# Loading V to every fourth partition, and ordering the score rows to match, in an attention kernel

## Chip, cores and metric

One core of a Trainium2 chip. The metric is device time in microseconds (us) of the whole kernel. Ratios compare runs of the same rounds on the same chip.

## The reference

Plain softmax attention over B x H = 512 heads, with 192 queries, 1024 keys and head dimension 128, all in bfloat16:

```python
B, H, Sq, Sk, D = 16, 32, 192, 1024, 128
def reference(q, k, v):
    scale = q.shape[-1] ** -0.5
    scores = jnp.einsum("bhqd,bhkd->bhqk", q, k) * scale
    p = jax.nn.softmax(scores, axis=-1)
    return jnp.einsum("bhqk,bhkd->bhqd", p, v)
```

q, k and v are normal numbers times 0.05, so the scores are tiny and each softmax row is nearly flat.

## The kernel before

The kernel works on pairs of heads; there are 256 pairs. Inputs come from HBM (the chip's main memory) into tiles in SBUF (on-chip memory of 128 partitions); the tensor engine writes its results to PSUM (a second on-chip memory). The scores are computed transposed, keys on the partitions, so the exponentials can serve directly as stationary operands of the second matmul. For that, the keys on the partitions of the scores and the rows of V on the partitions of V must be in the same order. One queue (SP) issues all transfers in a fixed order. K, q and the reordered V have four slots each (R = 4), V as loaded has ten (NVS = 10).

```python
    def load_k(p):
        if p >= R:
            e.wait_ge(s_tr, 2 * (p - R) + 2)
        e.dma_start(
            kn[:, p % R, :],
            kf[2 * p:2 * p + 2].rearrange("x (m s) d -> (x m) (s d)", s=2 * T),
        ).then_inc(s_kn[p % R], 16)
    def load_v(p):
        if p >= NVS:
            e.wait_ge(s_pv, p - NVS + 1)
        for w in range(2):
            e.dma_start(
                vs[64 * w: 64 * w + 64, p % NVS, :, :],
                vf[2 * p:2 * p + 2].rearrange("x (m w t) d -> w m x (t d)", w=2, t=T)[w],
            ).then_inc(s_v[p % NVS], 16)
# ... the loop that issues transfers, after a head that loads K and q of 4 pairs and V of 10
    for n in range(NPR + 2):
        if n + R < NPR:
            load_k(n + R)
            load_q(n + R)
        if n >= 2 and n - 2 + NVS < NPR:
            load_v(n - 2 + NVS)
        if n >= 3 and (n - 2) % GP == 0:
            store((n - 2) // GP - 1)
```

A partition of `kn` holds 16 rows of K, 4 KB. A partition of `vs` holds 8 rows of V, 2 KB for each head: transfer w = 0 of a pair fills partitions 0 to 63, w = 1 fills 64 to 127. POOL (GpSimd) copies V to a padded tile, with a column of ones for the row sums. The tensor engine transposes K in half steps (y = 0, 1), DVE (VectorE) copies each half out of PSUM, and one step of the tensor engine is two half steps of scores, transposes and the second matmul:

```python
    for p in range(NPR):
        gp.wait_ge(s_v[p % NVS], 32 * (p // NVS + 1))
        if p >= R:
            gp.wait_ge(s_pv, p - R + 1)
        gp.tensor_copy(
            vp[:, p % R, :, 0:D].bitcast(U32),
            vs[:, p % NVS, :, :].rearrange("p x (t d) -> p (x t) d", d=D).bitcast(U32),
        ).then_inc(s_vp, 1)
# ... tensor engine; `take` waits for a semaphore and counts it back
    def tr(p, y):
        if y == 0:
            take(s_kn[p % R], 16)
        if (p, y) != (0, 0):
            take(s_ev, 1)
        ins = None
        for t in range(T):
            for z in range(2):
                c0 = (8 * y + t) * D + 64 * z
                ins = pe.transpose(
                    k_ps[64 * z: 64 * z + 64, t * 128: t * 128 + 128],
                    kn[:, p % R, c0: c0 + 64], ident[:], tile_position=(0, 64 * z))
        ins.then_inc(s_tr, 1)
# ... inside qk(h), scores of one head
        for t in range(T):
            cut = {2: (0, 2, 3), 5: (0, 1, 3)}.get(t, (0, 3))
            for j0, j1 in zip(cut[:-1], cut[1:]):
                mv = qt[:, p % R, j0:j1, 64 * x: 64 * x + 64]
                c0 = t * SQ + j0 * 64
                for w in range(2):
                    ins = pe.matmul(
                        S[64 * w: 64 * w + 64, c0: c0 + (j1 - j0) * 64],
                        kt[:, p % R, 8 * w + t, 64 * x: 64 * x + 64], mv,
                        start=True, stop=True, tile_position=(0, 64 * w))
    def step(n):
        for x in range(2):
            if n < NPR:
                qk(2 * n + x)
            if n + 1 + x < NPR:
                tr(n + 1 + x, 1 - x)
            if n >= 2:
                pv(n - 2, 12 * x, 12 * x + 12)
```

## Time and profile before

| | before |
|---|---|
| time, median of the first 3 runs | 1199.38 us (1196.12 to 1203.05) |
| span of the profiled run, mean granted clock (share of TensorE's full clock) | 1197.7 us, 0.988 |
| PE (TensorE) busy | 995.0 us, 83% |
| ACT (ScalarE), DVE, POOL busy | 744, 546, 268 us |
| PE waiting ahead of the transposes of K | 186.0 us |

From the profile's page of the kernel before: busy time of each engine, then busy tenths in 40 equal slices of the span (DMA is the mean of the 16 DMA engines), then two groups of instructions (busy time and mean length of one, then idle time before them and what ended it), then the transfers (number, size, median us from issue to landing).

```profile
...
PE 995.0 (83%) x30722; PEld 947.9 (79%) x30722; DVE 546.4 (46%) x1031; ACT 744.1 (62%) x513; POOL 268.1 (22%) x263
...
PE   4598888888888888888888888888888888888885
...
DMA  9999999999999999999999999999999999999991
GB/s 211 230 257 264 284 264 279 277 273 277 282 278 268 277 271 279 275 278 272 280 278 274 277 279 266 281 279 267 285 277 269 284 272 274 275 271 277 274 294 40
...
L656 DVE COPY f_kt<-f_k 128x1024 bf16<-128x1024 bf16 x512 | 354.2, 692 | 623.6 <-PE f_k L569 623.5
L569 PE MATMUL f_k<-f_ident,f_kn 128*64 128x128 bf16 x8192 | 331.2, 221 | 186.2 <-PEq L558 186.0
...
f_kn<-in_k_dram SPq DMA_DIRECT2D x256, 512.0 KB, 9.9
f_vs<-in_v_dram SPq DMA_DIRECT2D x512, 256.0 KB, 9.2
...
```

PE has 17% of the span idle, and nearly all of it stands ahead of line 569, the transposes of K. PE's sequencer is named as the releaser, since a separate `take` on it waits for the K load. The DMA slices read 9 tenths throughout.

The view of waits says the same in totals (engine and line, what it waited for: us in total, times, longest):

```profile
...
PE f_k L569 <- PEq L558: 186.0, 245, 17.6
POOL f_vp L549 <- DMA f_vs<-in_v_dram: 18.6, 4, 9.3
...
```

In the timeline of PE (start, length, instructions; in brackets the idle time before), a half step is scores, transposes, second matmul:

```profile
...
602.54 0.86 PE L590 MATMUL f_s<-f_qt,f_kt 128*64 128x192 bf16 x20
603.21 0.64 PE L569 MATMUL f_k<-f_ident,f_kn 128*64 128x128 bf16 x16
603.65 0.90 PE L608 MATMUL f_o<-f_vp,f_pt 128*64 128x129 bf16 x24
604.36 0.86 PE L590 MATMUL f_s<-f_qt,f_kt 128*64 128x192 bf16 x20
605.55 0.64 PE L569 MATMUL f_k<-f_ident,f_kn 128*64 128x128 bf16 x16 [0.33 <-PEq L558]
605.99 0.90 PE L608 MATMUL f_o<-f_vp,f_pt 128*64 128x129 bf16 x24
606.69 0.86 PE L590 MATMUL f_s<-f_qt,f_kt 128*64 128x192 bf16 x20
...
```

The half step that starts at 602.54 runs without a wait and ends at 604.36: 1.82 us, so about 3.65 us for an undisturbed step of one pair (two half steps). In the next, the transposes start 0.5 us late. Over the span a pair takes 1197.7 / 256 = 4.68 us.

In a steady stretch, as a table by stretch (us of the stretch; busy us and instructions of PE, its weight loads, DVE, ACT, POOL; granted clock; DMA share; GB/s):

```profile
...
60.00:360.00 300.00, 259.35 (x8100) 247.77 (x8094) 142.84 (x269) 195.95 (x136) 69.94 (x67) 1.00 1.07 274
...
```

The trace also records every DMA packet with its size and duration, and sizes tell the streams apart: q 256 B, output 768 B, V 2 KB, K 4 KB. Sums are divided by 16 engines.

| stream | packets | MB | sum / 16, us | median ns |
|---|---|---|---|---|
| V | 65,536 | 134.2 | 628.5 | 159 |
| K | 32,768 | 134.2 | 407.4 | 164 |
| q | 98,304 | 25.2 | 110.9 | 18 |
| output | 32,768 | 25.2 | 88.9 | 36 |

V costs 1.54 times what K costs for the same bytes, at 134.2 MB / 628.5 us = 214 GB/s.

### The profile page before, as it was taken

The page shows a single profiled execution, that of the slowest core. Times are in us where ns is not written, and L with a number is a line of the kernel's source. Part 1 is how long each engine was busy: PE and PEld are TensorE (multiplying, and loading weights), DVE is VectorE, ACT ScalarE, POOL GpSimd, SP SyncE. Part 2 cuts the span into 40 slices and gives each one's busy share as a digit, 9 for nine tenths or more (in the row PEclk, how much of TensorE's full clock was granted, in tenths as well). Part 3 has the DMA queues.
Part 4 walks back from the last instruction along what each step waited for, and adds up shares of the span by engine and source line. Part 5 has one row for each costly group of instructions (what it writes and reads, how often), then busy time and mean ns, then how long its engine had stood idle before and what let it go on. Part 6 is the DMA issues. An engine that isn't in the chain of part 4 may idle for free. (4 is left out here: it accounts for less than half of the span.)

```text
span 1197.7 us, 67883 instructions
## 1 busy us (share of the span) xinstructions
PE 995.0 (83%) x30722; PEld 947.9 (79%) x30722; DVE 546.4 (46%) x1031; ACT 744.1 (62%) x513; POOL 268.1 (22%) x263
## 2 busy tenths in 40 slices
PE   4598888888888888888888888888888888888885
PEld 3598888887888887887887887787887887878885
DVE  1254444444444444444444444444444444444443
ACT  3276666666666666666666665666666666666663
POOL 1122222222222222222222222222222222222220
PEclk9799999999999999999999999999999999999999
DMA  9999999999999999999999999999999999999991
GB/s 211 230 257 264 284 264 279 277 273 277 282 278 268 277 271 279 275 278 272 280 278 274 277 279 266 281 279 267 285 277 269 284 272 274 275 271 277 274 294 40
DMA packets 250932, 319.39 MB, mean 267 GB/s; under 512 B 119808, under 2 KB 152576, under 8 KB 250880
## 3 DMA queue, kind: packets, MB, share of 16 engines
q1 hardware_dynamic: 250880, 318.85, 104.6%
q8 instruction: 13, 0.21, 0.1%
q14 instruction: 39, 0.32, 0.1%
HBM read 268.44 MB, written 25.17 MB: 245 GB/s over the span
## 5 line engine op out<-in xcount | busy, mean ns | idle before, releaser
L707 ACT ACTIVATE f_pt<-f_s 128x1536 bf16<-128x1536 f32 x512 | 742.8, 1451 | 439.2 <-PE f_s L590 439.2
L656 DVE COPY f_kt<-f_k 128x1024 bf16<-128x1024 bf16 x512 | 354.2, 692 | 623.6 <-PE f_k L569 623.5
L569 PE MATMUL f_k<-f_ident,f_kn 128*64 128x128 bf16 x8192 | 331.2, 221 | 186.2 <-PEq L558 186.0
L549 POOL COPY f_vp<-f_vs 128x1024 uint32<-128x1024 uint32 x256 | 267.2, 1044 | 908.9 <-PE f_o L608 890.3
L608 PE MATMUL f_o<-f_vp,f_pt 128*64 128x129 bf16 x12288 | 459.3, 221 | 2.2 <-PEq L558 2.2
L569 PEld LDWEIGHTS f_k<-f_ident,f_kn 128*64 128x64 bf16 x8192 | 276.1, 110 | 232.1 <-issue 232.0
L590 PE MATMUL f_s<-f_qt,f_kt 128*64 128x192 bf16 (+2 forms) x10240 | 444.4, 231 | 5.2 <-issue 5.2
L608 PEld LDWEIGHTS f_o<-f_vp,f_pt 128*64 128x64 bf16 x12288 | 395.8, 110 | 2.7 <-issue 2.7
L590 PEld LDWEIGHTS f_s<-f_qt,f_kt 128*64 128x64 bf16 x10240 | 360.4, 111 | 5.7 <-issue 5.7
L671 DVE TENSOR_TENSOR f_ob<-f_o,f_rinv 128x384 bf16<-128x384 f32 x256 | 142.7, 557 | 8.9
L667 DVE RECIPROCAL f_rinv<-f_o 128x3 f32<-128x3 f32 x256 | 46.3, 181 | 11.0 <-PE f_o L608 8.5
L707 ACT ACT_TABLE_LOAD x1 | 1.3, 1283 | 0.8 <-PEq L733 0.8
L640 PE MATMUL f_o<-f_bad,f_ones 128*1 128x1 bf16 x1 | 0.2, 164 | 1.4 <-DVEq L696 1.4
L640 PEld LDWEIGHTS f_o<-f_bad,f_ones 128*1 128x1 bf16 x1 | 0.1, 79 | 1.6 <-DVEq L696 1.6
L680 DVE TENSOR_TENSOR f_chk<-f_chk,f_rinv 128x750 f32<-128x750 f32 (+1 forms) x2 | 1.1, 558 | 0.1
L681 DVE TENSOR_REDUCE f_bad<-f_chk 128x1 bf16<-128x750 f32 (+1 forms) x2 | 1.1, 555 | 0.1
L679 DVE TENSOR_SCALAR f_chk<-f_rinv 128x750 f32<-128x750 f32 (+1 forms) x2 | 1.0, 509 | 0.0
L541 POOL TENSOR_SCALAR_AFFINE_SELECT f_ident<-f_ones 128x128 bf16<-128x128 bf16 x1 | 0.3, 294 | 0.1
L698 DVE CAST redo<-f_o 1x1 int32<-1x1 f32 x1 | 0.1, 146 | 0.3 <-PE f_o L641 0.3
L539 POOL MEMSET f_ones<- 128x128 bf16 x1 | 0.2, 205 | 0.3 <-POOLq L733 0.3
L544 POOL MEMSET f_vp<- 128x128 bf16 x1 | 0.2, 213 | 0.0
L733 POOL MEMSET const-float32-0.0<- 128x1 f32 x1 | 0.1, 99 | 0.3 <-issue 0.3
(5 smaller groups left out, 0.5 us busy)
## 6 DMA issues: line engine op xcount, KB each, us to landing
f_kn<-in_k_dram SPq DMA_DIRECT2D x256, 512.0 KB, 9.9
f_vs<-in_v_dram SPq DMA_DIRECT2D x512, 256.0 KB, 9.2
out_dram<-f_ob SPq DMA_DIRECT2D x64, 384.0 KB, 9.5
f_qt<-in_q_dram SPq DMA_TRANSPOSE x256, 9.9
```

The lines of the kernel that those rows point to most:

```text
L549: gp.tensor_copy(vp[:, p % R, :, 0:D].bitcast(U32), vs[:, p % NVS, :, :].rearrange("p x (t d) -> p (x t) d", d=D).bitcast(U32),).then_inc( ...
L569: ins = pe.transpose(k_ps[64 * z: 64 * z + 64, t * 128: t * 128 + 128], kn[:, p % R, c0: c0 + 64], ident[:], tile_position=(0, 64 * z))
L590: ins = pe.matmul(S[64 * w: 64 * w + 64, c0: c0 + (j1 - j0) * 64], kt[:, p % R, 8 * w + t, 64 * x: 64 * x + 64], mv, start=True, stop=True ...
L608: ins = pe.matmul(o_ps[64 * x: 64 * x + 64, j * 129: j * 129 + 129], pt[:, (2 * p + x) % NP, t * SQ + j * 64: t * SQ + j * 64 + 64], vp[:, ...
L640: pe.matmul(o_ps[0:1, 0:1], ones[:, 0:1], bad[:, 0:1], start=True, stop=False)
L656: dve.tensor_copy(kt[:, p % R, 8 * y: 8 * y + 8, :], k_ps[:].rearrange("d (t c) -> d t c", c=128),).then_inc(s_ev, 1)
L667: dve.reciprocal(ri, O[:, :, 128]).then_inc(s_rc, 1)
L671: dve.tensor_tensor(ob[:, so, a, :].rearrange("p (j d) -> p j d", j=3), O[:, :, 0:128], ri.unsqueeze(2).to_broadcast([128, 3, D]), ALU.mul ...
L679: done(dve.tensor_scalar(chk[:, lo:hi], rinv[:, lo:hi], 1.0 / RS_HI, 1.0 / RS_LO, ALU.max, ALU.min))
L680: done(dve.tensor_tensor(chk[:, lo:hi], chk[:, lo:hi], rinv[:, lo:hi], ALU.not_equal))
L681: done(dve.tensor_reduce(bad[:, i: i + 1], chk[:, lo:hi], mybir.AxisListType.X, ALU.max))
L707: act.activation(pt[:, h % NP, :], s_ps[h % 2][:], ACT_FN.Exp, scale=scale).then_inc(s_exp, 1)
```

## The change

The intent: each transfer of V should reach partitions all over the SBUF instead of one half of them. V comes in units of two pairs (four heads). Transfer c of four writes partitions c, c+4, ..., c+124, so partition 4m+2a+b holds the 8 rows from 32m+16b+8a. K stays loaded in 4 KB pieces. For its columns to follow this order, a transpose writes its 64 keys of one head as 32 pairs of neighbouring bfloat16 columns, each pair 8 bytes from the next. Number and size of packets, number of transfers, and all instruction counts of PE, DVE, ACT and POOL stay as they are.

```diff
# ... (hunks that only rename constants are left out)
@@ -453,10 +453,10 @@
 
             kn = sb("f_kn", [128, R, 2 * T * D], BF16)
 
-            kt = sb("f_kt", [128, R, 2 * T, 128], BF16)
+            kt = sb("f_kt", [128, R, T, 2, 128], BF16)
             qt = sb("f_qt", [128, R, 3, 128], BF16)
 
-            vs = sb("f_vs", [128, NVS, 2, T * D], BF16)
+            vs = sb("f_vs", [128, NV2, 4, T * D], BF16)
             vp = sb("f_vp", [128, R, 2 * T, VB], BF16)
             pt = sb("f_pt", [128, NP, T * SQ], BF16)
             ob = sb("f_ob", [128, NSO, GP, 3 * D], BF16)
@@ -489,14 +489,15 @@
                         qf[2 * p:2 * p + 2].rearrange("g (p j) d -> (g p) (j d)", j=3),
                     ).then_inc(s_q[p % R], 16)
 
-                def load_v(p):
-                    if p >= NVS:
-                        e.wait_ge(s_pv, p - NVS + 1)
-                    for w in range(2):
+                def load_v(u):
+                    if u >= NV2:
+                        e.wait_ge(s_pv, 2 * (u - NV2) + 2)
+                    for c in range(4):
                         e.dma_start(
-                            vs[64 * w: 64 * w + 64, p % NVS, :, :],
-                            vf[2 * p:2 * p + 2].rearrange("x (m w t) d -> w m x (t d)", w=2, t=T)[w],
-                        ).then_inc(s_v[p % NVS], 16)
+                            vs[c:128:4, u % NV2, :, :],
+                            vf[4 * u:4 * u + 4].rearrange(
+                                "x (m b a t) d -> a b m x (t d)", b=2, a=2, t=T)[c // 2, c % 2],
+                        ).then_inc(s_v[u % NV2], 16)
 
                 def store(g):
                     so = g % NSO
@@ -519,15 +520,15 @@
                 for p in range(2, R):
                     load_k(p)
                     load_q(p)
-                    load_v(p - 1)
-                for p in range(R - 1, min(NVS, NPR)):
-                    load_v(p)
+                for u in range(1, min(NV2, NPR // 2)):
+                    load_v(u)
                 for n in range(NPR + 2):
                     if n + R < NPR:
                         load_k(n + R)
                         load_q(n + R)
-                    if n >= 2 and n - 2 + NVS < NPR:
-                        load_v(n - 2 + NVS)
+                    u = (n - 3) // 2 + NV2
+                    if n >= 3 and n % 2 == 1 and u < NPR // 2:
+                        load_v(u)
                     if n >= 3 and (n - 2) % GP == 0:
                         store((n - 2) // GP - 1)
                 store(NPR // GP - 1)
@@ -543,12 +544,14 @@
                 ).then_inc(s_set, 1)
                 gp.memset(vp[:, :, :, D:VB], 1.0).then_inc(s_set, 1)
                 for p in range(NPR):
-                    gp.wait_ge(s_v[p % NVS], 32 * (p // NVS + 1))
+                    u, x = divmod(p, 2)
+                    if x == 0:
+                        gp.wait_ge(s_v[u % NV2], 64 * (u // NV2 + 1))
                     if p >= R:
                         gp.wait_ge(s_pv, p - R + 1)
                     gp.tensor_copy(
                         vp[:, p % R, :, 0:D].bitcast(U32),
-                        vs[:, p % NVS, :, :].rearrange("p x (t d) -> p (x t) d", d=D).bitcast(U32),
+                        vs[:, u % NV2, 2 * x: 2 * x + 2, :].rearrange("p x (t d) -> p (x t) d", d=D).bitcast(U32),
                     ).then_inc(s_vp, 1)
 
             @block.tensor
@@ -563,11 +566,14 @@
                     if (p, y) != (0, 0):
                         take(s_ev, 1)
                     ins = None
-                    for t in range(T):
+                    for i in range(8):
+
+                        kp = k_ps[:, 256 * (i % 4): 256 * (i % 4) + 256].rearrange(
+                            "d (m a b) -> d m a b", a=2, b=2)
                         for z in range(2):
-                            c0 = (8 * y + t) * D + 64 * z
+                            c0 = (8 * (i // 4) + 4 * y + i % 4) * D + 64 * z
                             ins = pe.transpose(
-                                k_ps[64 * z: 64 * z + 64, t * 128: t * 128 + 128],
+                                kp[64 * z: 64 * z + 64, :, i // 4, :],
                                 kn[:, p % R, c0: c0 + 64], ident[:], tile_position=(0, 64 * z))
                     ins.then_inc(s_tr, 1)
 
@@ -589,7 +595,7 @@
                             for w in range(2):
                                 ins = pe.matmul(
                                     S[64 * w: 64 * w + 64, c0: c0 + (j1 - j0) * 64],
-                                    kt[:, p % R, 8 * w + t, 64 * x: 64 * x + 64], mv,
+                                    kt[:, p % R, t, x, 64 * w: 64 * w + 64], mv,
                                     start=True, stop=True, tile_position=(0, 64 * w))
                     ins.then_inc(s_qk, 1)
 
@@ -654,8 +660,8 @@
                     if p >= R:
                         dve.wait_ge(s_qk, 2 * (p - R) + 2)
                     dve.tensor_copy(
-                        kt[:, p % R, 8 * y: 8 * y + 8, :],
-                        k_ps[:].rearrange("d (t c) -> d t c", c=128),
+                        kt[:, p % R, 4 * y: 4 * y + 4, :, :],
+                        k_ps[:].rearrange("d (t x c) -> d t x c", x=2, c=128),
                     ).then_inc(s_ev, 1)
 
                 def onorm(p):
```

More of the change, by code (lines that the diff above doesn't have):

```diff
@@ L393, in _ @@
                     exp_first(u)
+HINT = False
 RS_LO = 2.0 ** -40
@@ L399, with _attention_kernel @@
 PE_LOOP = 4
-HINT = False
-def _attention_kernel(nc, q, k, v, out, NVS=10):
+def _attention_kernel(nc, q, k, v, out, NV2=5):
     B, H, SQ, D = q.shape
@@ L431, in _attention_kernel @@
         s_q = [sem("f_q%d" % i) for i in range(R)]
-        s_v = [sem("f_v%d" % i) for i in range(NVS)]
+        s_v = [sem("f_v%d" % i) for i in range(NV2)]
         s_st = [sem("f_st%d" % i) for i in range(NSO)]
```

## The prediction

> **What bounds the kernel now: the DMA engines, through K.** In the page's slices DMA is at 9 tenths or more throughout (q1: 104.6% of 16 engines' span), PE busy 83%. In the view of waits PE stands 186 us, nearly all ahead of the transposes of K (line 569), waiting for a K load. In the timeline an unstalled step of one pair takes about 3.65 us; the span over 256 pairs is 4.68. ACT needs 2.9 us per pair (2 x 1.45), DVE 2.1, POOL 1.04: none binds.
>
> **Where the DMA time goes.** The trace's packets, summed over 16 engines: V 628 us (65,536 of 2 KB, median 159 ns), K 407 us (32,768 of 4 KB, median 164), q 111, output 89. The same 134 MB cost V 1.54 times what they cost K. A pair's V load lasts 2.27 us (median; 230 GB/s), its K load 1.71. [...] The K packets after V took 310 to 340 ns [...]; a K load after an output took 159 ns throughout (about 410 GB/s). [...]
>
> **What the change does.** Each V transfer writes 32 partitions, four apart, over the whole 0..127[...]. Bytes, packets and number of transfers stay, as do the counts on PE, DVE, ACT, POOL. V comes as 1 MB per two pairs; buffers hold ten pairs as before. The transposes write pairs of columns 8 bytes apart in PSUM instead of a solid run; unstalled, 16 issue in 0.42 us now. [...]
>
> **Cost.** If V ran like clean K, 80 ns per packet: V 1.3 us and K 1.3 [...], q 0.38, output 0.35: an estimate of 3.3 us of DMA per pair, below PE's 3.65. Then PE bounds: 256 x 3.65 + some 30 us of head and tail + a few stalls: about 975. [...]
>
> **Prediction: 1005 us, 80% range 962 to 1190.** Faster by over 2%: 0.80; within 2%: 0.15; slower: 0.05.
>
> **What would show it.** Right: V packets' median near 80 ns, V under 420 us of 16 engines; K's slow group (300 ns and over) gone; PE's wait ahead of line 569 from 186 us to under 50; DMA slices below 9 tenths; PE over 95% busy. Transposes: 16 still in 0.42 us, DVE copy 692 ns.
>
> **What would make it wrong.** V packets stay near 159 ns ([...] a limit on the HBM side, the source being now 2 KB every 8 KB): no change. Transposes at half speed: +0.84 us per pair on PE, near 1190. A lower granted clock with busier PE (0.988 now). The 1 MB bursts of V holding K back in the one queue.

The sum is V 1.3 + K 1.3 + q 0.38 + output 0.35 = 3.3 us of DMA per pair (80 ns is half of the 159 that a 4 KB packet of K took after an output; a q load lasted 0.37 us in the trace, though q's packets sum to 0.43 per pair), below PE's 3.65; so 256 x 3.65 = 934 us, with head, tail and stalls about 975. Cut after it are two slower cases: half of the gain, with V 1.8 and K 1.45, so 4.0 us per pair and some 1050 us, and no gain, 1195. They lifted the forecast from 975 to 1005 us and the top of its range to 1190. How likely they were, and that the new order of the columns would cost little, were guesses.

## More of the kernel before

The batches of experiments ran on different chips, so figures from the profiles (packets, waits) are also set side by side across chips; the kernel before took 1199.07 to 1199.85 us (medians) on all of them.

In the one V load that I followed, at 600.8 us, the first 64 of its 256 packets took 84 ns each and the rest 118 to 247 (median 166); the first 32 K packets after it took 313 to 358 ns.

## The result

| | before | after |
|---|---|---|
| time, median | 1199.53 us (4 runs) | 988.26 us (986.07 to 993.17, 4 runs) |
| ratio, 95% interval | | 0.8244 [0.8205, 0.8283] |
| span, granted clock | 1197.7 us, 0.988 | 986.6 us, 0.992 |
| PE busy | 995.0 us, 83% | 948.6 us, 96% |
| V packets: sum / 16, median | 628.5 us, 159 ns | 396.7 us, 86 ns |
| K packets: sum / 16, median | 407.4 us, 164 ns | 366.5 us, 160 ns |
| K packets of 300 ns and over | 6,072 | 977 |
| output packets: sum / 16, median | 88.9 us, 36 ns | 125.3 us, 36 ns |

The same lines from the page of the kernel after:

```profile
...
PE 948.6 (96%) x30722; PEld 944.2 (96%) x30722; DVE 546.1 (55%) x1031; ACT 744.2 (75%) x513; POOL 267.9 (27%) x263
...
PE   4699999999999999999999999999999999999995
...
DMA  9899999999999999999999999999999999999981
GB/s 272 240 287 342 356 328 334 336 355 332 343 325 350 332 337 347 338 344 316 335 353 343 328 331 358 335 345 322 342 319 357 319 354 341 334 326 351 342 263 38
...
L662 DVE COPY f_kt<-f_k 128x1024 bf16<-128x1024 bf16 x512 | 354.0, 691 | 412.8 <-PE f_k L575 412.8
...
L575 PE MATMUL f_k<-f_ident,f_kn 128*64 128x128 bf16 x8192 | 330.5, 220 | 22.8 <-PEq L561 22.7
...
f_kn<-in_k_dram SPq DMA_DIRECT2D x256, 512.0 KB, 5.7
f_vs<-in_v_dram SPq DMA_DIRECT2D x512, 256.0 KB, 4.5
...
```

PE reads 9 tenths in nearly every slice, and its idle time ahead of the transposes (now line 575) fell from 186.2 to 22.8 us. One transpose still takes 220 ns, one DVE copy 691 ns. Landing times about halved (K 9.9 to 5.7 us, V 9.2 to 4.5). But the DMA slices still read 9 tenths.

The waits:

```profile
...
PE f_k L575 <- PEq L561: 22.7, 15, 10.3
POOL f_vp L552 <- DMA f_vs<-in_v_dram: 16.3, 2, 10.6
...
```

Of the 22.7 us, 10.3 are one wait in the head, before 31 us, which stays. Between 50 and 950 us the sum is 2.3.

The timeline of PE:

```profile
...
601.88 0.86 PE L596 MATMUL f_s<-f_qt,f_kt 128*64 128x192 bf16 x20
602.55 0.64 PE L575 MATMUL f_k<-f_ident,f_kn 128*64 128x128 bf16 x16
603.02 0.89 PE L614 MATMUL f_o<-f_vp,f_pt 128*64 128x129 bf16 x24
603.73 0.86 PE L596 MATMUL f_s<-f_qt,f_kt 128*64 128x192 bf16 x20
604.39 0.64 PE L575 MATMUL f_k<-f_ident,f_kn 128*64 128x128 bf16 x16
604.84 0.90 PE L614 MATMUL f_o<-f_vp,f_pt 128*64 128x129 bf16 x24
605.54 0.86 PE L596 MATMUL f_s<-f_qt,f_kt 128*64 128x192 bf16 x20
...
```

No bracket is left. From 601.88 to 605.54 a whole step takes 3.66 us, the length of an undisturbed step of before. The steady stretch:

```profile
...
60.00:360.00 300.00, 299.50 (x9783) 298.94 (x9780) 173.22 (x327) 236.45 (x164) 85.55 (x82) 1.00 1.06 338
...
```

PE went from 259.35 to 299.50 busy us of 300, and about the same DMA share (1.06 against 1.07) now moves 338 GB/s rather than 274.

### The profile page after: what moved, and what is told of

Read it like the earlier page. It is cut to its first block, busy times and chain, and to the rows that moved or that the text cites. A ratio compares the mean times of both kernels' runs of the same rounds, so it can differ in the third digit from the quotient of the medians.

```text
span 986.6 us, 67757 instructions
## 1 busy us (share of the span) xinstructions
PE 948.6 (96%) x30722; PEld 944.2 (96%) x30722; DVE 546.1 (55%) x1031; ACT 744.2 (75%) x513; POOL 267.9 (27%) x263
## 5 line engine op out<-in xcount | busy, mean ns | idle before, releaser
L575 PE MATMUL f_k<-f_ident,f_kn 128*64 128x128 bf16 x8192 | 330.5, 220 | 22.8 <-PEq L561 22.7
L575 PEld LDWEIGHTS f_k<-f_ident,f_kn 128*64 128x64 bf16 x8192 | 286.7, 111 | 26.0 <-issue 25.7
```

The source lines that it names most:

```text
L575: ins = pe.transpose(kp[64 * z: 64 * z + 64, :, i // 4, :], kn[:, p % R, c0: c0 + 64], ident[:], tile_position=(0, 64 * z))
```

## The experiments

"Wrong on purpose" means that rows of V no longer match the scores. The comparison with the reference nevertheless passed in e1, e2, e3, e8 and e9, because the softmax is nearly flat; it failed only where V of other heads was used (e5, relative error 1.29). So this comparison doesn't vouch for the order of rows. For the changed kernel I checked the order apart from the chip: filling the index of each key through the transposes' and the loads' access patterns gives the same table for both. The theory that the expectations put to the test is that V's rate depends on which partitions one transfer covers: slow within one half of the 128 (and slower still for 16 neighbours), fast when spread over all. The runs show rates for sets of partitions.

### e1: neighbouring partitions again

```diff
-vs[c:128:4, u % NV2, :, :],
+vs[32 * c: 32 * c + 32, u % NV2, :, :],
```

> The changed kernel, with one thing put back: each of the four V transfers writes 32 neighbouring partitions (32c to 32c+31[...]) instead of every fourth one. HBM reads, packets, transfers, order of issue and all the engines' work are those of the changed kernel; the result is wrong on purpose. Theory [...]: V packets back to a median near 159 ns, PE's wait ahead of the K transposes back to 150 to 200 us, 1180 to 1210 us. Rival 1 (the order of HBM reads, 2 KB every 8 KB, was the gain) and rival 2 (four transfers for two pairs, fewer and larger groups, was the gain): stays within 2% of 988 us, V packets near 86 ns.

Measured: 1223.47 us (ratio to before 1.0191 [1.0171, 1.021]). V packets' median 169 ns, sum 669.5 us of 16 engines, or 200 GB/s. PE's wait is back:

```profile
...
PE f_k L575 <- PEq L561: 202.9, 108, 19.1
POOL f_vp L552 <- DMA f_vs<-in_v_dram: 20.4, 2, 12.4
...
```

The one edit, which leaves reads, packets, issues and engine work alone, gives the whole gain back. Neither the order of HBM reads nor the grouping by two pairs is the cause. The time came out 14 us above my range, and 24 us above before. Two things go that way in the records, and I didn't part them. V packets under 110 ns are 12.0% here against 22.6% before; in the load of before that I followed they were its first 64, and loads twice as long have fewer beginnings. And the mean granted clock is 0.958 against 0.988, with PE waiting less often but longer (108 waits, not 245).

### e2: the kernel before, every second partition

```diff
-vs[64 * w: 64 * w + 64, p % NVS, :, :],
+vs[w:128:2, p % NVS, :, :],
```

> The kernel before, with one thing changed: the two V transfers of a pair write partitions w, w+2, w+4, ... (64 partitions over the whole 0..127[...]) instead of 64w to 64w+63. HBM reads (2 KB every 4 KB), two transfers per pair, order of issue as before; result wrong on purpose. Theory [...]: V packets' median 80 to 100 ns, 985 to 1010 us. Rivals 1 and 2 (read order; grouping by two pairs): no change, 1190 to 1210 us, V packets near 159 ns. [...]

Measured: 981.33 us, ratio 0.8181 [0.8167, 0.8194]; V packets' median 87 ns. The destination alone carries the gain, with reads, transfers and grouping of the kernel before. Its ratio is slightly better than the changed kernel's (0.8239 in e5's rounds below, on another chip). Its V packets have a longer tail (mean 111 ns, 90th percentile 133, against 97 and 95 in the changed kernel), so some packets are still slow, but PE isn't held up: 300.00 us busy of 300 in the steady stretch.

### e8: apart, but in one half

```diff
-vs[c:128:4, u % NV2, :, :],
+vs[64 * (c // 2) + c % 2: 64 * (c // 2) + 64: 2, u % NV2, :, :],
```

> The changed kernel, with the V transfers writing every second partition of one half: 0,2..62; 1,3..63; 64,66..126; 65..127. Spread out[...]; result wrong on purpose. Theory [...]: as slow as with 32 neighbouring partitions, 1180 to 1210 us, V packets near 159 ns. Rival 3 (what counts is that the partitions of a transfer are apart[...]): near 988 us, or clearly between.

Measured: 1224.54 us, V packets' median 169 ns: the same as e1, and again 14 us above the range. That partitions lie apart is worth nothing here (169 ns in e8 and e1); that each transfer stays within one half of the SBUF is what counts (86 ns in the changed kernel, where it doesn't).

### e9: 16 neighbouring partitions

```diff
-for c in range(4):
+for c in range(8):
-    vs[c:128:4, u % NV2, :, :],
-    vf[...].rearrange("x (m b a t) d -> a b m x (t d)", b=2, a=2, t=T)[c // 2, c % 2],
+    vs[16 * c: 16 * c + 16, u % NV2, :, :],
+    vf[...].rearrange("x (h m b a t) d -> h a b m x (t d)", h=2, ...)[c % 2, c // 4, (c // 2) % 2],
# POOL waits for 128, not 64, per unit
```

> The changed kernel, with eight V transfers for two pairs, each to 16 neighbouring partitions[...]; same packets of 2 KB; result wrong on purpose. Theory [...]: V at about 110 GB/s, median of its packets about 300 to 330 ns; an estimate per pair is V 4.8 us, K 1.9, q and output 0.75, so 7.2 to 7.5 us, some 1800 to 1950 us. If [...] V were held by something else, it would stay near 1200 us.

Measured: 1698.1 us, ratio 1.4151. V packets' median 302 ns, as expected; 2048 B / 302 ns x 16 engines = 108 GB/s. (The 110 GB/s expected is about half of the 214 measured before; that 16 partitions would halve the rate was the author's assumption.) The total was over-estimated: 11.6% of V packets took under 110 ns, so V's sum was 1113 us (121 GB/s, or 4.35 us per pair rather than 4.8), and K's 456 (1.78 rather than 1.9). This run also makes twice as many V issues, as e4 below does; but e4 alone takes 1243 us and its V packets keep a median of 85 ns, so the issues do not explain these packets. Neighbouring ranges of 64 partitions (before), 32 (e1) and 16 (e9) give V packets of 159, 169 and 302 ns, and the sets spread over all 128 give 86 or 87: the rate does not follow the number of partitions alone (32 give 169 ns as neighbours and 86 spread over all; 64 give 159 and 87). Nor does it go with the width of the range: e1's sets are 32 wide and e8's 63, and both give 169 ns. Why 16 neighbours are that much slower than 32, when 32 are hardly slower than 64, the runs don't show. A set that lies in both halves without lying all over the SBUF (such as 0 to 31 with 64 to 95) was not run.

### e3: the order of K alone

The transposes, the copy and the score matmuls of the changed kernel, with the V loads of before.

```diff
 # the kernel before, with
+kp = k_ps[:, 256 * (i % 4): 256 * (i % 4) + 256].rearrange("d (m a b) -> d m a b", a=2, b=2)
-k_ps[64 * z: 64 * z + 64, t * 128: t * 128 + 128],
+kp[64 * z: 64 * z + 64, :, i // 4, :],
 # and kt, its copy and qk indexed as in the change
```

> The kernel before with the other half of the change alone: the transposes of K write pairs of columns, the scores follow that order; V is loaded as before, so the rows of V no longer match (wrong on purpose). Theory: no part of the gain and no cost: 1190 to 1205 us, transposes 16 in 0.42 us when not waiting, V packets' median near 159 ns. Rival (the new order itself frees the tensor engine or costs it something): outside 1185 to 1215 us.

Measured: 1199.78 us, ratio 0.9993 [0.9974, 1.0013]; V packets' median 159 ns, PE's wait 187.3 us. The other half of the change has no time of its own here. In this kernel PE waits, which could hide a small cost; that none appears where PE binds is read from the changed kernel, whose transposes take 220 ns and whose step takes 3.66 us. The order is there for correctness. This is one pattern, in which every two neighbouring columns stay together; single columns apart were not run.

### e4: four transfers for one pair

```diff
-vf[4 * u:4 * u + 4].rearrange(
+vf[2 * u:2 * u + 2].rearrange(
 # vs with 10 slots of 2 heads, one unit per pair; the waits follow
```

> The changed kernel, with the loads of V made for one pair at a time: four transfers of 128 KB (32 partitions, every fourth, two heads) per pair instead of four of 256 KB per two pairs. [...] correct result. Twice as many V issues on SP. In the changed kernel one V issue keeps SP 0.64 us, K 0.55, q 1.22, output 0.15 per pair. Theory A (an issue costs the same whatever its size): SP needs 4.5 us per pair, above PE's 3.66, so SP bounds: 1120 to 1170 us. Theory B (issue cost follows the number of packets, half here): 3.2 us per pair, below PE: 985 to 1000 us, and the grouping by two pairs was not needed.

Measured: 1242.82 us, ratio 1.0358 [1.033, 1.0386], correct: slower than the kernel before, with the sets of partitions of the changed kernel. The timeline of SP (start, length, transfers issued):

```profile
...
602.58 0.58 SPq L479 DMA_DIRECT2D f_kn<-in_k_dram  x1
603.21 1.22 SPq L487 DMA_TRANSPOSE f_qt<-in_q_dram  x1
604.48 2.55 SPq L496 DMA_DIRECT2D f_vs<-in_v_dram  x4
607.07 0.59 SPq L479 DMA_DIRECT2D f_kn<-in_k_dram  x1
...
```

From 602.58 to 607.07 is one pair: 4.49 us of issuing back to back, and 0.63 more for the output every fourth. Four V issues take 2.55 us, 0.64 each with the gap between two, as in the changed kernel although each moves half the bytes. Here is the median from issue to landing:

```profile
...
f_kn<-in_k_dram SPq DMA_DIRECT2D x256, 512.0 KB, 4.8
f_vs<-in_v_dram SPq DMA_DIRECT2D x1024, 128.0 KB, 3.5
...
```

A K load lands 4.8 us after issue, against 9.9 before, yet PE waited 215 us for K: the wait is for the issue, not for the transfer. The smaller transfers cost some DMA time too (V's packets sum to 560.6 us of 16 engines, against 398.5 in the changed kernel of the same rounds, at a median of 85 ns), but K landed sooner all the same. Theory A's cost of an issue holds, theory B falls. My range was too low: (4.49 + 0.63 / 4) x 256 = 1189 us without the head, since I had left out the gaps between issues and the head and tail; SP also waited some 125 us for engines between 60 and 1180 us, part of it beside that sum, and how the two combine I did not settle. The grouping by two pairs is thus needed with four transfers, though it brings nothing itself.

### e5: the changed kernel with hardly any V

```diff
-if n >= 3 and n % 2 == 1 and u < NPR // 2:
+if False:
 # POOL waits for V only for the first five units
```

> The changed kernel, with V loaded only for the first ten pairs and then used again (wrong on purpose): 96% of V's traffic and of its issues taken away. Theory (PE bounds the changed kernel between head and tail, 3.66 us per pair): 975 to 986 us, at most 1% less than the changed kernel, PE's share 96 to 97%. Rival (DMA, whose slices still read 9 tenths, still bounds it or shares in it): 940 to 965 us.

Measured: 982.92 us, ratio 0.8194 [0.8176, 0.8212]; the changed kernel in the same rounds 990.28 us, 0.8239 [0.8215, 0.8264]. From the page, and the steady stretch:

```profile
...
DMA  9676777777777677666666666776677676666651
GB/s 289 195 199 194 189 207 196 189 205 199 186 204 199 191 201 201 188 200 204 188 198 204 191 197 205 191 196 204 191 195 205 190 194 205 190 195 204 190 165 37
...
```

```profile
...
60.00:360.00 300.00, 300.00 (x9825) 300.00 (x9822) 173.50 (x328) 237.28 (x164) 85.53 (x82) 1.00 0.71 197
...
```

With 40% fewer bytes the DMA slices drop to 6 or 7 tenths, and the time by 0.5% (0.8194 / 0.8239). So PE bounds the changed kernel, and a DMA row of nines there does not mean that DMA bounds it. About 7 us are all that V's traffic still costs.

### e7: V held back in the head

```diff
-for u in range(1, min(NV2, NPR // 2)):
-    load_v(u)
+load_v(1)
-u = (n - 3) // 2 + NV2
-if n >= 3 and n % 2 == 1 and u < NPR // 2:
+u = (n + 3) // 2
+if n >= 1 and n % 2 == 1 and u < NPR // 2:
```

> The changed kernel, with V held back: the first two units are loaded at the start, unit u later in iteration 2u-3 of the issuing loop, rather than all five units ahead of the fifth K. Correct result. Theory (the head's one wait of 10.3 us ahead of the K transposes is K standing behind 4 MB of V in the one queue): that wait falls to under 3 us, 975 to 982 us in all. Rival (the head is bound by the sum of bytes, or V then comes late and PE stalls in the middle): 986 us or more.

Measured: 987.07 us, ratio 0.8235 [0.8209, 0.8261], against 0.8239 of the changed kernel: no difference shown over five runs each (the two profiled runs differ by 5 us of span). The longest wait ahead of the transposes fell from 9.5 to 4.5 us, not to under 3, and the waits ahead of the scores in the first 60 us are 5.9 us (4.3 in the changed kernel). My forecast of the gain fails: holding V back shortens that one wait, and the time hardly shows it.

### e10: another way to all partitions

Both K and V are loaded in natural order: partition p holds rows 8p to 8p+7. Then no column order is needed, and V of a pair is a single transfer.

```diff
 # the kernel before, with
-kf[2 * p:2 * p + 2].rearrange("x (m s) d -> (x m) (s d)", s=2 * T),
+kf[2 * p:2 * p + 2].rearrange("x (m s) d -> m x (s d)", s=T),
-for w in range(2):
-    vs[64 * w: 64 * w + 64, p % NVS, :, :],
-    vf[...].rearrange("x (m w t) d -> w m x (t d)", w=2, t=T)[w],
+vs[:, p % NVS, :, :],
+vf[2 * p:2 * p + 2].rearrange("x (m t) d -> m x (t d)", t=T),
-kt[:, p % R, 8 * w + t, 64 * x: 64 * x + 64], mv,
+kt[:, p % R, 8 * x + t, 64 * w: 64 * w + 64], mv,
 # POOL waits for 16, not 32, per pair
```

> The kernel before with another way [...], correct by construction: K is loaded as 128 partitions of 8 rows for each of the two heads (2 KB pieces, one transfer of 512 KB per pair), so that partition p holds rows 8p to 8p+7 for K and V alike, no column order is needed, and V of a pair is one transfer of 512 KB over all 128 partitions. Two V issues fewer per two pairs than the changed kernel. Theory ([...] PE then binding): V packets' median 80 to 90 ns, 978 to 986 us, that is level with the changed kernel or up to 1% better. Rival (2 KB pieces are slow for K as well, or 512 KB transfers starve the queue): over 992 us.

Measured: 982.97 us, ratio 0.8194 [0.8178, 0.8211], correct; the changed kernel in the same rounds 989.37 us, 0.8234 [0.8218, 0.8251]. That is 0.5% better, a small difference with intervals that do not meet, and it is simpler. K in 2 KB pieces costs little: K and V packets together have a median of 86 ns, and PE is 300.00 us busy of 300 in the steady stretch.

### e11: the same, with V asked for three pairs ahead

```diff
 # e10, with
-for p in range(R - 1, min(NVS, NPR)):
-    load_v(p)
-if n >= 2 and n - 2 + NVS < NPR:
-    load_v(n - 2 + NVS)
+if n + 3 < NPR:
+    load_v(n + 3)
```

> The same, with V asked for three pairs ahead rather than ten, so that only three V loads stand ahead of the fifth K at the start. Theory (part of the head's wait is K behind V in the one queue, part the issuing time of SP, which has one V issue per pair here): PE's wait ahead of the K transposes in the first 60 us falls from 16 us in the kernel with ten to 3 to 8 us, 970 to 979 us in all. Rival (the head is bound by bytes, or V now arrives too late in the middle): 980 us or more.

Measured: 982.35 us, ratio 0.8183 [0.8168, 0.8199]: level with e10. PE's wait ahead of the transposes in the first 60 us fell from 15.9 to 7.0 us as expected, but that ahead of the scores rose from 2.4 to 7.8. The rival holds: the order of loads in the head moves the wait, and hardly shortens it. What bounds the head is left open.

Two more runs of the changed kernel gave the comparisons of the same rounds.

> The changed kernel again, on the same chip as the three others, for pairs of the same rounds: 985 to 992 us.

Measured: 990.28 us (984.38 to 990.7).

> The changed kernel again, in the same rounds as the two alternatives: 984 to 991 us.

Measured: 989.37 us (986.98 to 992.4).

## Why the prediction was right

- **What bounded the kernel: right.** PE waited 186 us for K; e2 and e1, one edit each, take the wait away and bring it back.
- **Why V was slow: shown as a pattern, not as a mechanism.** What the runs show is that transfers within one half of the partitions are slow and transfers spread over all are fast: V's sums give 214 and 200 GB/s for 64 and 32 neighbours (before, e1), 121 for 16 (e9, where 11.6% of V packets took under 110 ns), and 338 for every fourth partition of all 128.
- **V's packets: right.** "Near 80 ns" measured 86, "under 420 us" 396.7.
- **What stays: right.** Packets, instructions and the length of transposes (221 and 220 ns; 16 start within 0.42 us in both) and copies (692 and 691) are unchanged, and e3 shows that writing pairs 8 bytes apart costs nothing measurable (0.9993).
- **PE then bounds: right.** 3.65 us per pair was predicted, 3.66 measured; "under 50" us of waiting ahead of the transposes measured 22.7, and "over 95% busy" 96%. e5 confirms it. But the prediction got there by comparing 3.3 us of DMA per pair with PE's 3.65, and that comparison failed (see "DMA slices" below): that the conclusion held was partly luck.
- **Only half of the gain, or none: not seen.** This fear lifted the point from 975 to 1005 and the top of the range to 1190; 988 was measured. How the DMA engines share the work can't be read, as the records don't say which of them wrote what.
- **"DMA slices below 9 tenths": wrong.** They stayed at 9. The estimate of 3.3 us of DMA per pair took clean packets; the sums per pair are V 1.55, K 1.43, output 0.49 and q 0.43, together 3.90 us. That is more than PE's 3.66, and close to the 4.0 for which the author expected some 1050 us; yet the kernel took 988. So a sum of packet times is no lower bound of the time here: it passes even the 3.85 us of span per pair (986.6 / 256). Medians are nearly clean, so a minority of long packets makes the excess; plainest in the output, where 769 packets took over 180 ns, up to 2.6 us, and before none did. It did not bind, as e5 shows. Why these packets are long is open. The long output packets go with loading V by two pairs: 743 to 786 in the four profiles with V spread (after, its two repeats, e7), 100 or 101 in e1, e8 and e9, and none or one in e2, e3, e4 and e10.
- **"K's slow group gone": mostly.** 977 of 6,072 are left. The count alone doesn't show that V held K up: e5, with hardly any V, has 3,770 such packets (median 596 ns), nearly all among the first 32 of a K load, and is no slower for it.
- **"A lower granted clock with busier PE": not so.** It was 0.992 against 0.988, and lowest, 0.844, in e9, where PE waits most (531 us ahead of the transposes).

## What to carry to other kernels

When two streams of equal bytes take different DMA time, compare their packets in the trace, and look at which partitions each single transfer covers: a set spread over all 128 partitions, even every fourth, can run faster than a solid half (here 338 against 214 GB/s by the packets' sums, 86 against 159 ns by their medians). Count the issuing queue too: four small transfers per pair made the same good pattern slower than the bad one (e4's 1243 us against 1199). A DMA row of nines, or a sum of packet times above the span, is no proof that DMA bounds; take bytes away and see.
